# A transformer block, forward and backward: forward attention by chunks of 512 queries, the MLP of a chunk issued inside the next chunk's attention

## The chip, the cores and the metric

One core of one Trainium2 chip. The time is the device time of one launch in microseconds. Lower is better.

## The reference

One block on x of 2048 positions and 512 channels: attention with 32 heads of 16, and an MLP of 1792 hidden units with a squared ReLU. Both are modulated by six vectors from c. The kernel returns the output and the gradients of the nine inputs that take part.

```
mod = (silu(c) @ w_mod).reshape(1, 6, 1, -1)       # sa, ca, ga, sb, cb, gb
h = layernorm(x) * (1 + ca) + sa
q, k, v = split(h @ wqkv)                          # 32 heads of 16
x = x + ga * ((softmax(q @ k.T * 16**-0.5) @ v) @ wo)
h = layernorm(x) * (1 + cb) + sb
r = relu(h @ w1 + b1)
x = x + gb * ((r * r) @ w2 + b2)
out, vjp = jax.vjp(block, x, wqkv, wo, w1, b1, w2, b2, c, w_mod)
return out, *vjp(grad_out)
```

## The kernel before

Matmul operands are bfloat16, sums are float32 in PSUM, and positions are tiled by 128 (S, 16 tiles) or by 512 (four chunks). A quad is four heads whose 16 channels are padded to 32, so that a quad fills 128 partitions; there are eight. The program runs in stages, one behind the other:

- phase0: the six modulation vectors.
- phase12: first LayerNorm (x is loaded on SP's queue, L313), transposes, the V products (tm_group) and Q, K of quad 0 (fm_group: four matmuls of 512 columns, L281), then forward attention. The loop is over 16 pairs of heads, and within a pair over the four chunks of 512 queries, and within that over 16 blocks of 128 keys: 1024 units. A unit is two QK matmuls (L410) into a score buffer `st` of 128x1024, one exp on ScalarE (L413), and eight PV matmuls of 17 columns (L419) into `accbank`. 64 groups of 16 units share a PSUM bank: at a group's end VectorE takes two reciprocals (L428) and two products (L429), casts the group's output (L433) and clears the accumulator for the next group (L406). Three buffers hold scores. 120 further Q, K, V groups are put between the units at even steps. K comes to the chip once for each quad (L469), the masked Q per pair (L462), both on SP's queue. Each engine's order is the scheduler's.
- phase3: O is transposed on TensorE, then output projection (L523), second LayerNorm, fc1 (L547, with the ReLU on ScalarE, L549), square (L550), fc2 (L556).
- phase4: MLP backward: du (L652, with the product on VectorE, L654), dx (L661), the backward of the second LayerNorm (L578 to L590), dO (L940) and the padded, transposed copies of dO for the attention backward (L943 to L970). The weights are first transposed on TensorE (L570).
- phase45: weight gradients of the MLP and of wo; phase5: attention backward; phase6: the gradients through QKV and the modulation.

The operations of phases 3 and 4 depend on the attention's output of all heads of a position, and of nothing else in the attention.

Of the kernel before, what the change touches and what calls it, by code (L numbers as in the profile page):

```python
# [23 lines left out]
def chunks(total, size):  # L24
    out = []
    s = 0
    while s < total:
        w = min(size, total - s)
        out.append((s, w))
        s += w  # L30
    return out


class K:
# [29 lines left out]
    def build(self, ctx: ExitStack):  # L64
# [21 lines left out]
        self.stash = False  # L86
        if self.stash:
            self.put_d = self.dram("put_d", [NQ * 2 * self.SC * ST, P, 2, 512], BF16)

        stop = self.opts.get("stop_after", 99)  # L90
        self.dmaq = [nc.gpsimd]
        self.dmai = 0
        self.open_pools = {}
        phases = [self.phase0, self.phase12, self.phase12b, self.phase3, self.phase4, self.phase45, self.phase5, self.phase6, self.phase7]
        for i, ph in enumerate(phases):
            ph()
            if stop <= i:
                break
        for name in list(self.open_pools)[::-1]:
            self.close_pool(name)  # L100

    def phase12b(self):
        pass
# [11 lines left out]
    def phase0(self):  # L115
# [13 lines left out]
        self.e16 = pp.tile([P, 1], F32, name="e16")  # L129
        self.e1617 = pp.tile([P, 1], F32, name="e1617")  # L130
        nc.vector.memset(self.e16[:], 0.0)
        nc.vector.memset(self.e1617[:], 0.0)
        one11 = pp.tile([1, 1], F32, name="one11")
        nc.vector.memset(one11[:], 1.0)
        for j in range(4):
            nc.sync.dma_start(self.e16[32 * j + 16:32 * j + 17, :], one11[:])
            nc.sync.dma_start(self.e1617[32 * j + 16:32 * j + 17, :], one11[:])
            nc.sync.dma_start(self.e1617[32 * j + 17:32 * j + 18, :], one11[:])
# [7 lines left out]
        self.selmaskV = pp.tile([P, 64], F32, name="selmaskV")  # L146
        nc.gpsimd.memset(self.selmaskV[:], 0.0)
        for j in range(4):
            nc.gpsimd.affine_select(
                out=self.selmaskV[32 * j:32 * j + 16, :], in_=self.selmaskV[32 * j:32 * j + 16, :],  # L150
                compare_op=ALU.not_equal, fill=1.0, base=-16 * ((j + 2) % 4), pattern=[[1, 64]], channel_multiplier=-1)

        self.mod_bc = pp.tile([P, 6 * D], F32, name="mod_bc")
# [3 lines left out]
        with tc.tile_pool(name="p0", bufs=1) as sb, tc.tile_pool(name="p0ps", bufs=2, space=PSUM) as ps:  # L157
            cT_b = sb.tile([P, DT], BF16, name="cT_b")
# [19 lines left out]
            for (n0, nw) in chunks(6 * D, 512):  # L178
                pt = ps.tile([P, 512], F32, name="modps")
                for kt in range(DT):  # L180
                    nc.tensor.matmul(pt[:, :nw], lhsT=sc_bc[:, kt, :], rhs=wmod[:, kt, n0:n0 + nw],
                                     start=(kt == 0), stop=(kt == DT - 1))
                nc.vector.tensor_copy(self.mod_bc[:, n0:n0 + nw], pt[:, :nw])
            junk = sb.tile([P, P], F32, name="junk")
            for j in range(6):
                for t in range(DT):
                    nc.vector.scalar_tensor_tensor(
                        junk[:], self.mod_bc[:, j * D + t * P:j * D + (t + 1) * P], 1.0, self.ident_f[:],
                        ALU.mult, ALU.mult, accum_out=self.modT[:, j * DT + t:j * DT + t + 1])
        self.opcaT = pp.tile([P, DT], F32, name="opcaT")  # L190
# [3 lines left out]
        if "mod_bc" in self.dbg:  # L194
            nc.sync.dma_start(self.dbg["mod_bc"], self.mod_bc[:])
            nc.sync.dma_start(self.dbg["modT"], self.modT[:])

    def mod_row(self, j):
        D = self.D
        return self.mod_bc[:, j * D:(j + 1) * D]  # L200
# [53 lines left out]
    def phase12(self):  # L254
        tc, nc, pp, io = self.tc, self.nc, self.pp, self.io
        S, D, H, NQ, ST, DT = self.S, self.D, self.H, self.NQ, self.ST, self.DT
        self.rstd1 = pp.tile([P, ST], F32, name="rstd1")
        self.rl = pp.tile([P, ST, H], F32, name="rl")
        KB = ST
        po = self.open_pool("pO", bufs=1)  # L260
        self.O_tm = po.tile([P, ST, D], BF16, name="O_tm")
        self.wo_3 = po.tile([P, DT, D], BF16, name="wo3")
        with tc.tile_pool(name="p12", bufs=1) as sb, tc.tile_pool(name="p12e", bufs=8) as eb:
            xhat1T = sb.tile([P, DT, S], BF16, name="xhat1T")
            Vaug = sb.tile([P, ST, H, DH + 1], BF16, name="Vaug")
            nc.gpsimd.memset(Vaug[:, :, :, DH:DH + 1], 1.0)
            wq = sb.tile([P, DT, 3 * D], BF16, name="wqkv")
            nc.scalar.dma_start(wq[:], io["A_wqkv"].rearrange("(kt p) n -> p kt n", p=P))
            bias_bc = sb.tile([P, 3 * D], F32, name="bias_bc")
            bcol = sb.tile([P, 3 * NQ], F32, name="bcol")  # L270
            wpads = [sb.tile([P, DT, NQ, P], BF16, name=f"wpad{t}") for t in range(3)]
            for t in range(3):
                nc.gpsimd.memset(wpads[t][:], 0.0)
            dsts = [self.QTq_d, self.KTq_d, self.VTq_d]
            qtm_v = self.by_quad(self.qtm_d)
            ktm_v = self.by_quad(self.ktm_d)

            def fm_group(ps_pool, t, g, s0, sw, eng="vector"):
                pt = ps_pool.tile([P, 512], F32, name="pps")
                for kt in range(DT):  # L280
                    nc.tensor.matmul(pt[:, :sw], lhsT=wpads[t][:, kt, g, :], rhs=xhat1T[:, kt, s0:s0 + sw],  # L281
                                     start=(kt == 0), stop=(kt == DT - 1))
                ev = eb.tile([P, 512], BF16, name="ev_fm")
                bc = bcol[:, t * NQ + g:t * NQ + g + 1]
                if eng == "scalar":
                    nc.scalar.activation(ev[:, :sw], pt[:, :sw], ACT.Identity, bias=bc, scale=1.0)
                else:
                    nc.vector.tensor_scalar(ev[:, :sw], pt[:, :sw], bc, None, ALU.add)  # L288
                dq = self.dmaq[self.dmai % len(self.dmaq)]
                self.dmai += 1  # L290
                dq.dma_start(dsts[t][g, :, s0:s0 + sw], ev[:, :sw])

            def tm_group(ps_pool, st, t):
                pt = ps_pool.tile([P, 512], F32, name="pps")
                for kt in range(DT):
                    nc.tensor.matmul(pt[:, :D], lhsT=xhat1T[:, kt, st * P:(st + 1) * P], rhs=wq[:, kt, t * D:(t + 1) * D],
                                     start=(kt == 0), stop=(kt == DT - 1))
                if t < 2:
                    ev = eb.tile([P, D], BF16, name="ev_tm")
                    nc.vector.tensor_tensor(ev[:], pt[:, :D], bias_bc[:, t * D:(t + 1) * D], ALU.add)  # L300
                    dq = self.dmaq[self.dmai % len(self.dmaq)]
                    self.dmai += 1
                    with nc.allow_non_contiguous_dma(reason="128B runs"):
# [1192 lines left out]
```

## Time and profile before

| | |
|---|---|
| median of three runs | 3326.37 us (3326.18 to 3335.05) |
| profiled execution | 3329.45 us, its span 3327.6 us |
| granted TensorE clock, mean | 0.963 |
| busy: TensorE, VectorE, ScalarE, GpSimd | 2954.7, 1866.0, 2381.2, 231.7 us |
| startup, until the first exp | 0 to 93.3 us |
| forward attention, first to last exp | 93.3 to 1037.9 us |
| projection, MLP forward and backward, dO | 1037.9 to 1478 us |
| weight gradients | 1478 to 1653 us |
| attention backward | 1653 to 3153 us |

A line of the groups reads: code line, engine, operation, output and inputs by their names, count, then busy time and mean duration of one, then the idle time before it and what ended it. PEld is the loading of a matmul's stationary operand. Matmuls are pipelined: one of 512 columns is shown as 0.38 us, but in a run they follow one another sooner.

### The profile page before, as it was taken

The numbers are of one execution on the slowest core, as the hardware profiler recorded it, in microseconds if no ns is written. First come the engines' busy times: TensorE is split into PE (matmuls) and PEld (weight loads), VectorE is DVE, ScalarE is ACT, GpSimd is POOL, SyncE is SP. The second block draws the span as 40 slices with busy tenths as digits, with TensorE's granted clock in tenths as the row PEclk, the third lists the DMA queues.
The fourth block names the chain that finished last, engine by engine and source line by source line (L and its number), as shares of the span: only waits on it lengthen the run. The fifth ranks groups of instructions, "written<-read, shape, count | busy, mean of one in ns | idle before, by whom it ended". The sixth has DMA issues, their size and how long they took to land. (4 is left out here: it accounts for less than half of the span.)

```text
span 3327.6 us, 75207 instructions
## 1 busy us (share of the span) xinstructions
PE 2954.7 (89%) x31556; PEld 1438.8 (43%) x31556; DVE 1866.0 (56%) x2745; ACT 2381.2 (72%) x3577; POOL 231.7 (7%) x303
## 2 busy tenths in 40 slices
PE   5999998888885878849899999999999999999987
PEld 2455553333332334326544444444444444444433
DVE  6222220000001545626588888888888888888765
ACT  3899999999996223433377777777777777777633
POOL 3111220000002002431000000000000000000000
PEclk8999999999997889969999999999999999999998
DMA  3111110000004246564499999999999999999951
GB/s 124 64 51 48 46 51 12 6 13 12 6 2 146 81 141 203 138 203 148 130 192 189 203 187 206 193 204 195 192 201 190 206 191 205 191 188 184 206 170 62
DMA packets 1176799, 447.77 MB, mean 135 GB/s; under 512 B 1086346, under 2 KB 1142284, under 8 KB 1176460
## 3 DMA queue, kind: packets, MB, share of 16 engines
q1 hardware_dynamic: 1150556, 376.25, 56.3%
q0 software_dynamic: 17280, 57.03, 5.5%
q10 hardware_dynamic: 8624, 9.70, 0.9%
q8 instruction: 246, 4.03, 0.5%
q14 instruction: 93, 0.76, 0.1%
HBM read 106.83 MB, written 67.64 MB: 52 GB/s over the span
## 5 line engine op out<-in xcount | busy, mean ns | idle before, releaser
L1213 ACT ACTIVATE pu<-st 128x512 bf16<-128x512 f32 x2048 | 1132.7, 597 | 299.9 <-PE st L1211 298.1
L1218 DVE TENSOR_TENSOR ds<-dp,pu 128x1024 bf16<-128x1024 f32 x1024 | 1208.5, 1219 | 234.9 <-ACT pu L1213 226.9
L413 ACT ACTIVATE pu<-st 128x1024 bf16<-128x1024 f32 x1024 | 940.1, 1381 | 4.7 <-PE accbank L419 4.7
L1211 PE MATMUL st<-KTm,QTq 128*128 128x512 bf16 x2048 | 779.2, 380 | 14.9 <-ACT pu L1213 9.2
L1214 PE MATMUL dp<-VTm,dOTq 128*128 128x512 bf16 x2048 | 775.7, 379 | 7.5 <-DVE ds L1218 5.8
L1159 PEld LDWEIGHTS <-dsT 128*128 128x128 bf16 x8192 | 487.3, 96 | 490.3 <-DMA dsT<-ds 18.9
L410 PE MATMUL st<-QTm,KTq 128*128 128x512 bf16 x2048 | 606.9, 377 | 7.3 <-DMA KTq<-KTq_d 1.6
L1159 PE MATMUL accq<-Kg,dsT 128*128 128x16 bf16 x8192 | 493.7, 170 | 12.4 <-DMA dsT<-ds 12.3
L419 PEld LDWEIGHTS <-pu 128*128 128x128 bf16 x8192 | 291.9, 96 | 457.9 <-ACT pu L413 407.3
L419 PE MATMUL accbank<-Vaug,pu 128*128 128x17 bf16 x8192 | 353.9, 172 | 67.2 <-DVE accbank L406 7.5
L428 DVE RECIPROCAL rl<-accbank 128x4 f32<-128x4 f32 x128 | 23.0, 180 | 526.1 <-PE accbank L419 525.6
L1139 PE MATMUL acckv<-ds,Qg 128*16 128x512 bf16 x2048 | 309.1, 382 | 0.8 <-DVE ds L1218 0.7
L1139 PE MATMUL acckv<-pu,dOg 128*16 128x512 bf16 x2048 | 309.1, 382 | 0.0
L1211 PEld LDWEIGHTS <-QTq 128*128 128x128 bf16 x2048 | 196.0, 96 | 225.4 <-issue 220.6
L1214 PEld LDWEIGHTS <-dOTq 128*128 128x128 bf16 x2048 | 197.5, 96 | 36.1 <-DVE ds L1218 16.2
L288 DVE TENSOR_SCALAR ev_fm<-pps,bcol 128x512 bf16<-128x512 f32 x92 | 69.1, 751 | 195.9 <-PE pps L281 194.9
L410 PEld LDWEIGHTS <-KTq 128*128 128x128 bf16 x2048 | 130.0, 96 | 35.8 <-issue 20.5
L281 PE MATMUL pps<-xhat1T,wpad 128*128 128x512 bf16 x384 | 122.8, 378 | 4.9 <-DVE ev_fm L288 3.8
L1390 POOL DMA_DIRECT2D wmod<-in_w_mod_dram x6 | 4.5, 754 | 1553.7 <-DMA dsT<-ds 1519.8
L549 ACT ACTIVATE rT<-ups,bias 128x512 bf16<-128x512 f32 x56 | 38.5, 687 | 53.8 <-PE ups L547 53.8
L652 PE MATMUL daps<-gT,W2gbT 128*128 128x512 bf16 x224 | 58.5, 404 | 19.3 <-DVE duT L654 19.3
L725 ACT COPY a_blk<-trps 128x1024 bf16<-128x1024 bf16 x28 | 28.3, 1012 | 59.0 <-PE trps L722 58.9
(297 smaller groups left out, 2315.4 us busy)
## 6 DMA issues: line engine op xcount, KB each, us to landing
rT_d<-rT SPq DMA_DIRECT2D x4, 1792.0 KB
rT<-rT_d SPq DMA_DIRECT2D x4, 1792.0 KB
duT_d<-duT POOLq DMA_DIRECT2D x4, 1792.0 KB, 13.1
rT_f<-rT_d SPq DMA_DIRECT2D x14, 512.0 KB
duT_f<-duT_d POOLq DMA_DIRECT2D x14, 512.0 KB, 3.6
xhat_d<-xhat SPq DMA_DIRECT2D x2, 2048.0 KB
QTq_d<-ev_fm POOLq DMA_DIRECT2D x32, 128.0 KB, 2.1
QTm<-QTq_d SPq DMA_DIRECT2D x128, 32.0 KB
```

Source lines behind the costliest of these rows:

```text
L281: nc.tensor.matmul(pt[:, :sw], lhsT=wpads[t][:, kt, g, :], rhs=xhat1T[:, kt, s0:s0 + sw], start=(kt == 0), stop=(kt == DT - 1))
L288: nc.vector.tensor_scalar(ev[:, :sw], pt[:, :sw], bc, None, ALU.add)
L410: nc.tensor.matmul(stt[:, a, :qw], lhsT=KT[:, kb * P:(kb + 1) * P], rhs=QTm[a][:, q0:q0 + qw], start=True, stop=True)
L413: nc.scalar.activation(pu[:, :, :qw], stt[:, :, :qw], ACT.Exp, scale=self.scale)
L419: nc.tensor.matmul(acc[:, a, sub, :], lhsT=pu[:, a, sub * P:(sub + 1) * P], rhs=Vaug[:, kb, heads[a], :], start=False, stop=False, skip_gr ...
L652: nc.tensor.matmul(pt[:, :sw], lhsT=W2gbT[:, kt, ft * P:(ft + 1) * P], rhs=gT[:, kt, s0:s0 + sw], start=(kt == 0), stop=(kt == DT - 1))
L1139: nc.tensor.matmul(acckv[r:r + DH, :], lhsT=T[n][:, ib, col:col + DH], rhs=src[:, a, :], start=(ib == 0), stop=(ib == ST - 1))
L1159: nc.tensor.matmul(accq[:, ib, a, :], lhsT=dsT[:, (i * 2 + a) * 4 + sub, :], rhs=T["K"][:, 4 * c + sub, col:col + DH], start=(c == 0 and i ...
L1211: nc.tensor.matmul(stt[:], lhsT=T["QT"][:, q], rhs=masked["KT"][2 * jp + a][:, c0:c0 + 512], start=True, stop=True)
L1213: nc.scalar.activation(pu[:, a, :], stt[:], ACT.Exp, scale=self.scale)
L1214: nc.tensor.matmul(dp[:, a, :], lhsT=T["dOT"][:, q], rhs=masked["VT"][2 * jp + a][:, c0:c0 + 512], start=True, stop=True)
L1218: nc.vector.tensor_tensor(dsg[:, i], dp[:], pu[:], ALU.mult)
```

## The change

phase12, phase3 and phase4 become one stage, phase_fwd. Its loop is over four chunks of queries, within a chunk over the eight quads and their two pairs, and within a pair over the 16 blocks of keys: the same 1024 units, with all heads of a chunk done after 256 of them. TensorE's order is now written by hand: QK of unit n, PV of unit n−2, then a step of background work, which hands out matmuls from generators at a credit of 1.15 a unit. A generator can ask for a hold of some units (`yield ("wait", 9)`) to let an operand arrive. The background of chunk 0 is Q and K of quads 1 to 7; then the MLP weights; then, behind chunk c+1's attention, the whole of phases 3 and 4 for chunk c (260 matmuls of 512 columns). The last chunk's comes after the loop.

Other differences: `st` has two buffers instead of three, the background three PSUM banks. The transposes of O, of the normalised activations, of g, dx, dO and of the weights, and the position-major copies of Q, K and V, are DMA transposes on SP's queue instead of TensorE transposes or second products. V's padded product falls away. In hidden chunks ReLU, the LayerNorm backward and the scaling of the weights are VectorE's, and parts GpSimd's; in the last chunk ReLU and a part of the LayerNorm backward are ScalarE's, as before. K is loaded for each chunk and quad, 32 times instead of 8, and Q for each group; both on GpSimd's queue. The load of x stands in a pool that follows phase0's.

```diff
+class Background:
...
+    def step(self, rate):
+        if self.hold:
+            self.hold -= 1
+            return
+        self.credit = min(self.credit + rate, 2.0)
+        while self.gens and self.credit > 0:
+            r = self.next()
+            if r is None:
+                break
+            if isinstance(r, tuple):
+                self.hold = r[1]
+                break
+            self.credit -= max(r, 0.25)
...
-        phases = [self.phase0, self.phase12, self.phase12b, self.phase3, self.phase4, self.phase45, self.phase5, self.phase6, self.phase7]
+        phases = [self.phase0, self.phase_fwd, self.phase45, self.phase5, self.phase6]
...
+        def load_q(qc, g, jp):
+            for j in (2 * jp, 2 * jp + 1):
+                nc.gpsimd.dma_start(QTm[j][32 * j:32 * j + 32, :], self.QTq_d[g, 32 * j:32 * j + 32, 512 * qc:512 * (qc + 1)])
...
+        order = [(qc, g, jp) for qc in range(SC) for g in range(NQ) for jp in range(2)]
+        bg = Background()
+        bg.add(self.gen_qkv())
...
+        def pv(u):
+            (qc, g, jp, kb, acc, pu) = u
+            if kb == 0:
+                nc.vector.memset(acc, 0.0)
...
+            if (g, jp) == (NQ - 1, 1):
+                bg.add(self.gen_mlp(qc, self.take_o(qc, O32)))
...
+        with tc.manual_schedule(engines={mybir.EngineType.PE}):
+            for n, (qc, g, jp) in enumerate(order):
+                if (qc, g, jp) == (1, 0, 0):
+                    bg.drain()
+                    self.close_qkv()
+                    self.open_mlp()
+                    bg.add(self.gen_weights())
+                acc = accbank[:, n % 2]
+                for kb in range(ST):
+                    if kb == ST // 2 and n + 1 < len(order):
+                        load_q(*order[n + 1])
+                        if jp == 1:
+                            KTn = load_k(order[n + 1][1])
+                    stt = stp.tile([P, 2, 512], F32, name="st")
...
+                    nc.scalar.activation(pu[:], stt[:], ACT.Exp, scale=self.scale)
+                    pend.append((qc, g, jp, kb, acc, pu))
+                    if len(pend) > 2:
+                        pv(pend.pop(0))
+                    bg.step(1.15)
...
+        bg.drain()
+        self.close_mlp()
...
+    def gen_mlp(self, sc, O_b):
...
+        nc.sync.dma_start_transpose(OT[:].rearrange("p a b c -> p (a b) c"), O_b[:].rearrange("p a b -> p (a b)"))
...
+        nc.sync.dma_start_transpose(xhT[:].rearrange("p a b c -> p (a b) c"), xh[:].rearrange("p a b -> p (a b)"))
+        nc.gpsimd.dma_start(tm_v(self.xhat2_d), xh[:])
+        yield ("wait", 9)
...
+            if last:
+                nc.scalar.activation(rT[:, ft, :], pt[:], ACT.Relu, bias=self.bias1[:, ft:ft + 1], scale=1.0)
+            else:
+                nc.vector.tensor_scalar(rT[:, ft, :], pt[:], self.bias1[:, ft:ft + 1], 0.0, ALU.add, ALU.max)
...
+            if k:
+                yield from self.gen_do(sc, *todo.pop(0))
+        yield ("wait", 9)
+        yield from self.gen_do(sc, *todo.pop(0))
```

The order of instructions shows it at three places. First TensorE within a unit of the attention. Before, the two QK matmuls wait for an earlier PV (through the score buffer), and PV for the exp:

```order
L410 LDWEIGHTS KTq
L410 MATMUL st<-QTm_663,KTq 128x512 [waits PE_49]
L410 LDWEIGHTS KTq
L410 MATMUL st<-QTm_665,KTq 128x512
L419 LDWEIGHTS pu [waits Activation_49]
L419 MATMUL accbank<-Vaug,pu 128x17
...
```
After (auT is the squared ReLU, pps a background sum, L648 is fc2):

```order
L345 LDWEIGHTS KTq
L345 MATMUL st<-QTm_662,KTq 128x512 [waits Activation_49]
L345 LDWEIGHTS KTq
L345 MATMUL st<-QTm_664,KTq 128x512
L315 LDWEIGHTS pu
L315 MATMUL accbank<-Vaug,pu 128x17
...
L648 LDWEIGHTS auT
L648 MATMUL pps<-w_4901,auT 128x512
```
The wait for the exp has moved to the QK, a unit's PV comes after it without one, and a background matmul closes the unit.

Second, VectorE at a group's end. Before:

```order
L428 RECIPROCAL rl<-accbank 128x4 [waits DVE_49,PE_49]
L429 TENSOR_TENSOR O_660<-accbank,rl 128x4x16 [waits DVE_49]
L428 RECIPROCAL rl<-accbank 128x4
L429 TENSOR_TENSOR O_660<-accbank,rl 128x4x16 [waits DVE_49]
L433 CAST O_tm<-O_660 128x4x32 [waits DVE_49]
L406 MEMSET accbank 128x136
```
After, in the stretch where a hidden chunk's LayerNorm backward runs (lnb_nc to dx and dxb are its steps, dOp_t is dO):

```order
L702 TENSOR_SCALAR lnb_nc_8723<-lnb_s_8721 128x1 [waits DVE_49]
L704 TENSOR_SCALAR lnb_nc1r<-lnd_mv,rstd_5391 128x1 [waits DVE_49]
L706 SCALAR_TENSOR_TENSOR lnb_t<-xh_5608,lnb_nc_8723,pps 128x512 [waits DVE_49]
L322 RECIPROCAL rl<-accbank 128x4 [waits PE_49]
L709 SCALAR_TENSOR_TENSOR dx_8715<-lnb_t,rstd_5391,lnb_gp 128x512 [waits DMAHW2_49,DVE_49,Pool_49]
L323 TENSOR_TENSOR O_656<-accbank,rl 128x4x16 [waits DVE_49]
L681 CAST dxb<-dx_8715 128x512 [waits DMAHW1_49,DMASW3_49,DVE_49]
L322 RECIPROCAL rl<-accbank 128x4
L323 TENSOR_TENSOR O_656<-accbank,rl 128x4x16 [waits DVE_49]
L311 MEMSET accbank 128x136 [waits DVE_49]
L724 TENSOR_TENSOR dOp_t<-pps,rl 128x512 [waits PE_49]
```
The group's eviction and the clearing of the accumulator now stand between steps of the LayerNorm backward, one of which waits for GpSimd, and the cast of the group's output is gone.

Third, the queues at the start. SP before:

```order
L177 DMA wmod<-in_w_mod_dram 128x4x3072
...
L137 DMA e_91<-one_94 1x1 [waits DMAHW4_49]
L138 DMA e_91<-one_94 1x1 [waits DMAHW5_49]
L313 DMA x_269<-in_A_x_dram 128x16x512 [waits DMAHW6_49]
L316 DMA xhat_d<-xhat_271 128x16x512 [waits DMAHW0_49,Activation_49]
```
and after:

```order
L188 DMA wmod<-in_w_mod_dram 128x4x3072
L384 DMA x_246<-in_A_x_dram 128x16x512 [waits DMAHW0_49,DVE_49,DMAHW1_49,PE_49,Activation_49]
L387 DMA xhat_d<-xhat_248 128x16x512 [waits Activation_49]
L445 DMA QTq_d<-ev_fm 128x512 [waits DVE_49]
L447 DMA_TRANSPOSE ev_tm<-ev_fm 128x4x128
```
The load of x now waits for VectorE, ScalarE and TensorE. GpSimd's queue after, ahead of the first load of K (vpad is the padded copy of V, ktm_d the position-major K):

```order
L451 DMA ktm_d<-ev_tmc 128x256 [waits DMASW3_49,Pool_49]
L465 COPY vpad_228<-Vaug 128x8x2x16 [waits DMAHW5_49,DVE_49]
L466 COPY vpad_228<-Vaug 128x8x2x16
L465 COPY vpad_229<-Vaug 128x8x2x16 [waits DMAHW6_49,DVE_49]
L466 COPY vpad_229<-Vaug 128x8x2x16
L465 COPY vpad_228<-Vaug 128x8x2x16 [waits DMAHW7_49,DVE_49,Pool_49]
L466 COPY vpad_228<-Vaug 128x8x2x16 [waits Pool_49]
L468 DMA VTq_d<-vT 128x8x512 [waits DMAHW0_49]
L300 DMA KTq<-KTq_d 128x2048 [waits DMAHW1_49,DMASW5_49,DMAHW3_49,DVE_49,Activation_49]
```
In before the first load of K stands on SP's queue, right behind the first loads of Q.

More of the change, by code (lines that the diff above doesn't have):

```diff
@@ L258, in phase12 @@
         self.rl = pp.tile([P, ST, H], F32, name="rl")
[L259 to L267, printed above, removed]
-            nc.scalar.dma_start(wq[:], io["A_wqkv"].rearrange("(kt p) n -> p kt n", p=P))
[L269 to L279, printed above, removed]
```

1038 lines of the change are left out of this document (392 added, 646 removed).

## The prediction, made before the result was known

> **What bounds the kernel now.** I first read the busy time by stretches of the span, cut where the exps of the forward attention begin and end, where the MLP backward begins, where the weight gradients begin, and where the attention backward begins. Columns: length, then busy time and instruction count of each engine, the granted TensorE clock, the DMA share and GB/s.
>
> ```profile
> span 3327.6 us, 75207 instructions
> ...
> 0.00:93.30 93.30, 49.15 (x218) 21.75 (x219) 56.64 (x212) 29.57 (x37) 29.53 (x36) 0.84 0.38 128
> 93.30:1037.90 944.60, 867.46 (x10690) 398.66 (x10689) 155.44 (x495) 939.88 (x1024) 74.43 (x117) 1.00 0.08 26
> 1037.90:1236.00 198.10, 137.26 (x720) 63.07 (x720) 74.13 (x160) 55.16 (x71) 21.64 (x21) 0.84 0.43 149
> 1236.00:1478.00 242.00, 158.67 (x905) 79.33 (x906) 129.04 (x326) 90.91 (x213) 71.26 (x86) 0.81 0.60 179
> 1478.00:1653.00 175.00, 154.21 (x1632) 108.36 (x1630) 97.28 (x179) 55.52 (x55) 27.56 (x33) 0.98 0.43 132
> ```
>
> The second row is the forward attention: ScalarE, the fourth pair of numbers, is busy 939.88 of 944.60 us. The third and fourth rows are the phases for the output projection and MLP forward, and for the MLP backward: 198.1 + 242.0 = 440.1 us in which ScalarE is busy 146 us only. The two kinds of work stand one behind the other, and the change lays the second under the first. So the question is what room TensorE has in the attention. That is in the groups and in the timeline (start, duration, engine, line; in brackets the idle time before).
>
> ```profile
> L413 ACT ACTIVATE pu<-st 128x1024 bf16<-128x1024 f32 x1024 | 940.1, 1381 | 4.7 <-PE accbank L419 4.7
> ...
> L419 PEld LDWEIGHTS <-pu 128*128 128x128 bf16 x8192 | 291.9, 96 | 457.9 <-ACT pu L413 407.3
> ```
>
> ```profile
> 504.62 0.27 PEld L419 LDWEIGHTS <-pu 128*128 128x128 bf16 x8 [0.60 <-ACT pu L413]
> ...
> 504.84 0.59 PE L410 MATMUL st<-QTm,KTq 128*128 128x512 bf16 x2
> ...
> 505.54 0.27 PEld L419 LDWEIGHTS <-pu 128*128 128x128 bf16 x8 [0.60 <-ACT pu L413]
> ...
> 505.76 0.59 PE L410 MATMUL st<-QTm,KTq 128*128 128x512 bf16 x2
> ```
>
> The 1024 exps take 940.1/1024 = 0.918 us each, back to back, and a unit (one block of keys for a pair of heads and 512 queries) repeats in 505.54 − 504.62 = 0.92 us. TensorE waits for the exp's result in 407.3 us of the stage. Its eight PV matmuls take 504.84 − 504.62 = 0.22 us. A 512-wide matmul's issue time comes from a long run of them:
>
> ```profile
> 75.47 7.07 PE L281 MATMUL pps<-xhat1T,wpad 128*128 128x512 bf16 x32
> ```
>
> One alone takes 0.38, so (7.07 − 0.38)/31 = 0.216 us each. A unit thus holds TensorE for 0.22 + 2 × 0.216 = 0.65 us and leaves 0.27.
>
> **The change, term by term.** *Removed:* the 440.1 us stretch, of which a part comes back as the last chunk's tail.
>
> *Credit of 1.15 background matmuls a unit.* 0.65 + 1.15 × 0.216 = 0.90 us against 0.918: it fits, with 0.02 us to spare. ScalarE would go on setting the pace, but TensorE has next to nothing to catch up with. A stall in its queue that goes beyond the finished score tile ahead of ScalarE is paid in full. That tile is worth 0.918 − 0.59 (two QK matmuls) − about 0.08 (two semaphore gaps) = 0.25 us. Chunk 0's Q, K groups (224 matmuls) and three chunks of MLP (260 each), 1004 in all plus the bias ones, fit into 1024 × 1.15 = 1178 credits, so I expect all three to be done, but for the last four matmuls, when the attention ends.
>
> *Group boundary, 64 of them.* Before has it too, and this is what it looks like there:
>
> ```profile
> 524.79 0.36 PE L419 MATMUL accbank<-Vaug,pu 128*128 128x17 bf16 x8
> ...
> 525.20 0.19 DVE L428 RECIPROCAL rl<-accbank 128x4 f32<-128x4 f32 x1 [13.41 <-PE accbank L419]
> 525.42 0.23 DVE L429 TENSOR_TENSOR O<-accbank,rl 128x64 f32<-128x64 f32 x1
> 525.56 0.17 DVE L428 RECIPROCAL rl<-accbank 128x4 f32<-128x4 f32 x1
> ...
> 525.77 0.22 DVE L429 TENSOR_TENSOR O<-accbank,rl 128x64 f32<-128x64 f32 x1
> ...
> 526.02 0.23 DVE L433 CAST O_tm<-O 128x128 bf16<-128x128 f32 x1
> 526.28 0.17 DVE L406 MEMSET accbank<- 128x136 f32 x1
> ```
>
> The last PV run is issued by 524.79 + 0.22 = 525.01; the memset that the next PV waits for ends at 526.45. The chain is 1.44 us, and without the cast (0.26), which the change drops, 1.2 us. Before covers it with two further QK pairs from a third score buffer. After has two score buffers, and between the two PV runs stand only one background step (0.25) and one QK pair (0.43): 0.68. The stall is 1.2 − 0.68 = 0.5 us, of which the finished tile takes up between 0 and 0.25; I take 0.4, since at 0.02 us a unit the tile is only just rebuilt by the next boundary. 63 × 0.4 = **25 us**, with ends 0 (VectorE faster at it) and 35.
>
> *VectorE queue at boundaries.* VectorE now also works for the MLP, in order. Prices from before's MLP stretch:
>
> ```profile
> L654 DVE SCALAR_TENSOR_TENSOR duT<-daps,rT 128x512 bf16<-128x512 f32 x56 | 38.4, 688 | 29.3 <-PE daps L652 16.6 <-DMA rT<-rT_d 12.3
> ...
> L948 POOL TENSOR_TENSOR prod<-dOp_t,o 128x512 f32<-128x512 bf16 x16 | 18.8, 1172 | 0.3
> ...
> L587 DVE SCALAR_TENSOR_TENSOR lnb_t<-xch,lnb_nc,lnb_dxh 128x512 f32<-128x512 bf16 x16 | 15.9, 992 | 0.3
> ...
> L581 DVE SCALAR_TENSOR_TENSOR lnb_junk<-lnb_dxh,xch 128x512 f32<-128x512 f32 x16 | 13.8, 864 | 11.2 <-ACT lnb_dxh L578 11.2
> L590 DVE SCALAR_TENSOR_TENSOR dx<-lnb_t,rstd,lnb_gp 128x512 f32<-128x512 f32 x16 | 12.7, 794 | 12.9 <-DMA dx_d<-dx 11.5 <-ACT lnb_gp L589 0.6
> ...
> L212 DVE BATCH_NORM_STATS2 ln_stats<-x 128x6 f32<-128x512 f32 x16 | 10.6, 669 | 0.0
> ...
> L217 DVE TENSOR_SCALAR xhat<-x,ln_mv,rstd 128x512 bf16<-128x512 f32 x16 | 7.4, 541 | 0.0
> ...
> L505 ACT ACTIVATE w<-w,opcbT 128x1792 bf16<-128x1792 bf16 x4 | 6.8, 1776 | 11.5 <-PE b1ps L488 11.5
> ```
>
> Where LN2's backward runs, a tile costs VectorE 0.67 + 0.86 + 0.99 + 0.79 = 3.3 us, plus a wait for a GpSimd pass near 1.17, and the order of the change weaves the eviction into it. Some 3 boundaries of each hidden chunk fall there; at 2.5 us each, 3 × 3 × 2.5 = **22 us** (ends 0, where the tile lies clear of the boundary, and 9 × 4.5 = 40). Elsewhere the background's VectorE work (0.69 us for four matmuls, which take 3.2 us) has room.
>
> *Waits of TensorE for a transposed operand.* TensorE's order is fixed, so a late operand also holds QK. The price of a DMA transpose is only in the attention backward:
>
> ```profile
> L1225 SPq DMA_TRANSPOSE dsT<-ds x256: 4699/5106/6867, 1662.8 to 3141.0; - x128
> ...
> L1159 PEld LDWEIGHTS <-dsT x76: 95/96/98, 1672.3 to 1684.8; 128*128 128x128 bf16 x76
> ```
>
> 32 blocks of 128x128 take 5.1 us of queue, 0.16 us a block, and the first was usable at most 1672.3 − 1662.8 = 9.5 us after its issue, so at most 4.4 after the queue's part. For the second LayerNorm's operand (16 blocks): add, statistics and four normalisations 0.7 + 0.9 + 4 × 0.54 = 3.8 us, then 2.6 + up to 4.4: 11 us against the 9 units (8.3 us) that the code holds back. That is up to 2.7 us, three times. The scaling of w1, once, is four passes near 1.78 us in front of a boundary: 7 us. Together I take **15 us** (0 to 30).
>
> The Trainium skill, "VectorE: DVE Perf Modes", section "The three transpose paths", speaks against moving transposes off TensorE: it gives 1309 ns for a 128x128 block by DMA and 390 ns on TensorE. The row above, 0.16 us a block in a run of 32, is eight times below that.
>
> *Startup.* In before the load of x is issued at 14.53, and the first exp comes at 93.3:
>
> ```profile
> 14.53 0.39 SPq L313 DMA_DIRECT2D x<-in_A_x_dram  x1
> ...
> 25.11 0.68 DVE L245 BATCH_NORM_STATS2 ln_stats<-x 128x6 f32<-128x512 bf16 x1
> ...
> 86.01 0.35 SPq L469 DMA_DIRECT2D KTq<-KTq_d  x1
> ...
> 91.29 1.47 PE L410 MATMUL st<-QTm,KTq 128*128 128x512 bf16 x6 [1.56 <-DMA KTq<-KTq_d]
> ```
>
> After, the load waits for work of VectorE, ScalarE and TensorE that in before ends about where the statistics start (25 us), so LayerNorm starts some 12 us later. K is then loaded by GpSimd's queue, behind copies that wait for the first transposes; Q and K are computed before V now, which gives some of it back. I take **+15 us** (0 to 25).
>
> *Tail.* Behind the last exp stand the last chunk's 260 matmuls and 4 left over: 264 × 0.216 = 57 us at full clock. Around them nothing fills TensorE: O's eviction, cast and transpose 8 us, LN2 and its transpose 10, the last LN backward, transpose and dO 9; and part of it runs at the lower clock that the MLP stretches had (0.81, 0.84), which I put at 4. **88 us.** Lower end 70 (full clock, weight gradients starting early), upper end 440.1/4 = 110, before's own price of a quarter.
>
> *Unchanged:* from the weight gradients on (1478 to the end) the code is the same. *Moved off for nothing:* TensorE's transposes and V groups, hidden behind the exp or gone with the 440 us.
>
> The profiled execution took 3329.45 us: 3329.45 − 440 + 25 + 22 + 15 + 15 + 88 = 3054; the median of the runs shown is 3 us below this execution, so **3051 us**.
>
> **Rivals.** *A: TensorE paces the loop.* With 0.02 us spare, a tenth of a microsecond more per unit (semaphore gaps of the fixed order, matmuls held by a product whose VectorE eviction is late) is not hidden: 1024 × 0.1 = 102 us, so 3153. For it: the spare is small, and there are two score buffers in place of three. Against it: in the attention backward TensorE runs as densely:
>
> ```profile
> 1653.00:3153.00 1500.00, 1452.58 (x16644) 704.04 (x16645) 1257.00 (x1113) 1151.40 (x2084) 1.81 (x3) 0.99 1.08 196
> ```
>
> 1452.58 of 1500 us at a granted clock of 0.99. Chance 0.20.
>
> *B: the stalls vanish.* VectorE's work falls clear of the boundaries, startup costs 5, the tail 75, stalls 15: 3326 − 440 + 95 = 2981. Against it: the chain above is a row, not a guess. Chance 0.16.
>
> *C: slower than before.* Each hidden chunk has five places where TensorE must wait for a transposed operand (the LN2 product, and four dO groups), the tail six: 21 in all. To eat 3326 − 3051 = 275 us, each must wait 13 us longer than in the sum, so a transpose would be some 22 us late instead of 9.5; at 25 us the kernel stands at 3051 + 21 × 16 = 3387. Queued behind one another and behind stores on one queue they might be that late; the DMA engines' share of 0.08 in the attention speaks against it. Chance 0.05. A milder form, 4 us longer each, gives 3051 + 84 = 3135; chance 0.05.
>
> By the page's 1309 ns, 16 blocks would take 20.9 us in place of 2.6, so the LN2 product would wait 18 us longer in each of four chunks, and O's transpose in the tail as much: 90 us, an estimate by that page, 3141. The row's 9.5 us for twice the blocks is against it.
>
> *D: no gain.* If the loads of Q and K, now in GpSimd's queue, are held there each time, all 64 groups lose; to lose the whole 275 us each would have to lose 4.3 us. The load is asked for 8 units (7.3 us) ahead and a transfer of that queue lands 2.0 us after its issue:
>
> ```profile
> KTq_d<-ev_fm POOLq DMA_DIRECT2D x32, 128.0 KB, 2.0
> ```
>
> So a hold of 7.3 − 2.0 + 4.3 = 9.6 us at every group would be needed. Chance 0.02.
>
> **How the numbers follow.** The forecast, 3020 to 3085, has 0.52. The range for 8 in 10 takes in B's centre and the lower half of A: 2980 to 3140. A measurement of this kernel tells 0.3% (10 us) from no change. Faster: 0.52 + 0.20 + 0.16 + 0.05 = 0.93; within 0.3%: 0.02 (D); slower: 0.05 (C).
>
> **What would show it.** Right: the exps span 985 to 1025 us in place of 944; idle time before the exp is put down to PV and memset, once in 16 exps; no MLP matmul but the last chunk's after the last exp; 80 to 95 us from there to the first weight gradient. First exp near 108. Wrong: gaps before the exp spread evenly over the units (A), long waits of TensorE for a DMA transpose (C) or for Q and K (D), or a change in the time of the attention backward.

## The result: 3142 us, 0.944 of the time before

The changed kernel takes 3142.47 us in the median of four runs (3136.24 to 3143.60), against 3327.52 for the kernel before (3326.18 to 3335.05): a ratio of 0.9436, 95% interval 0.9417 to 0.9455. The forecast of 3051 had the direction and the mechanism; the gain is 185 us where 275 were expected (3326 − 3051), and the time lies 57 us above the forecast's 3020 to 3085 and 2 us above the upper end of the wide range, 3140.

The profile after, in stretches (length, busy time and count of TensorE, weight load, VectorE, ScalarE, GpSimd; clock, DMA share, GB/s), cut at the first and the last exp of the forward attention, behind the last dO product, and shortly behind the first weight-gradient products:

```profile
0.00:104.30 104.30, 44.14 (x199) 19.58 (x203) 52.27 (x178) 29.84 (x36) 31.51 (x59) 0.76 0.50 145
104.30:1132.50 1028.20, 923.09 (x11079) 514.61 (x11281) 297.78 (x854) 959.51 (x1025) 225.28 (x419) 0.98 0.37 94
1132.50:1252.70 120.20, 66.89 (x268) 26.95 (x272) 51.62 (x142) 17.69 (x31) 24.64 (x40) 0.78 0.57 122
1252.70:1290.20 37.50, 12.41 (x43) 8.37 (x45) 17.97 (x31) 7.33 (x16) 18.79 (x18) 0.54 0.83 258
1290.20:1458.30 168.10, 144.56 (x1584) 102.82 (x1596) 92.26 (x164) 51.26 (x40) 15.21 (x26) 1.00 0.44 130
```

The attention stretch is 1028 us long where it was 945, and ScalarE is no longer busy in all of it. The groups of that stretch say why:

```profile
L348 ACT ACTIVATE pu<-st 128x1024 bf16<-128x1024 f32 x1024 | 959.6, 1041 | 68.7 <-PE st L345 57.7
...
L315 PE MATMUL accbank<-Vaug,pu 128*128 128x17 bf16 x8192 | 359.1, 171 | 64.6 <-DVE accbank L311 57.7
```

The exp waits 57.7 us for scores (4.7 us in all before), and PV waits 57.7 us for the memset of the accumulator. That the two sums are equal is chance; where the exps lose time has to be counted. I take 0.9165 us as the exp's own pace and add up by how much more than that lies between the ends of successive exps. The whole lag is 89.7 us, of which 59.2 us fall on one place, exp number 3 of a group of 16, counted from 0. PV runs two units late, so this is the exp behind the first QK that stands behind the new group's first PV. (By its place it is the group's fourth; the expectations below, and this text from here on, call it the third exp of a group.) In the kernel before the same count gives 6.2 us, 6.1 of them at that place.

The span adds up as follows, with each stretch against the same stretch before (the attention backward's first exp is at 1655.5 before, 1458.3 after):

| stretch | before | after | difference | forecast |
|---|---|---|---|---|
| up to the first exp | 93.3 | 104.3 | +11 | +15 |
| first to last exp | 944.8 | 1028.3 | +83.5 | +62 |
| last exp to the attention backward | 617.4 | 325.7 | −291.7 | −352 (−440 + 88) |
| attention backward | 1484.1 | 1493.6 | +9.5 | 0 |
| rest | 187.9 | 189.8 | +1.9 | 0 |

The third row holds two thirds of the miss. TensorE's own view of it (start, duration, what it did; in brackets the wait before it):

```profile
1135.62 1.89 PE L720 MATMUL pps<-wogaT,dxT 128*128 128x512 bf16 x4 [2.59 <-DMA dxT<-dxb]
1147.26 0.61 PE L616 MATMUL pps<-wo,fT 128*128 128x512 bf16 x1 [9.75 <-DMA fT<-O_b]
...
1168.75 13.56 PE L635 MATMUL pps<-fT,w 128*128 128x512 bf16 x56 [16.06 <-DMA fT<-xh]
...
1231.41 1.89 PE L720 MATMUL pps<-wogaT,dxT 128*128 128x512 bf16 x4 [17.19 <-DMA dxT<-dxb]
...
1247.67 1.89 PE L720 MATMUL pps<-wogaT,dxT 128*128 128x512 bf16 x4 [5.92 <-DMA dxT<-dxb]
...
1266.95 2.01 PE L826 MATMUL csbps<-diag,ones_f 128*128 128x128 f32 x6 [14.27 <-DVE dsb_part L846]
1279.30 6.96 PE L826 MATMUL csbps<-diag,ones_f 128*128 128x128 f32 x22 [10.35 <-DVE diag L824]
1286.05 0.63 PE L769 MATMUL g2ps<-g_tm,ones_b 128*128 128x512 bf16 x1
```

From the last exp to the last dO product are 120 us instead of 88, and then 37 us pass before the weight gradients are under way.

### The profile page after: what moved, and what is told of

Its sections match the earlier page's. It is cut to its first block, busy times and chain, and to the rows that moved or that the text cites. A ratio compares the mean times of both kernels' runs of the same rounds, so it can differ in the third digit from the quotient of the medians.

```text
span 3141.7 us, 73207 instructions
## 1 busy us (share of the span) xinstructions
PE 2765.5 (88%) x30278; PEld 1440.6 (46%) x30788; DVE 1866.1 (59%) x2741; ACT 2274.9 (72%) x3325; POOL 322.8 (10%) x569
## 5 line engine op out<-in xcount | busy, mean ns | idle before, releaser
L348 ACT ACTIVATE pu<-st 128x1024 bf16<-128x1024 f32 x1024 | 959.6, 1041 | 68.7 <-PE st L345 57.7
L1019 PE MATMUL dp<-VTm,dOTq 128*128 128x512 bf16 x1779 | 675.5, 380 | 7.9 <-DVE ds L1023 5.9
L345 PE MATMUL st<-QTm,KTq 128*128 128x512 bf16 x1938 | 592.9, 382 | 48.9 <-issue 13.8
L315 PEld LDWEIGHTS <-pu 128*128 128x128 bf16 x8192 | 355.3, 96 | 318.0 <-issue 86.5
L315 PE MATMUL accbank<-Vaug,pu 128*128 128x17 bf16 x8192 | 359.1, 171 | 64.6 <-DVE accbank L311 57.7
L345 PEld LDWEIGHTS <-KTq 128*128 128x128 bf16 x2048 | 193.0, 96 | 205.0 <-issue 147.2
L1019 PEld LDWEIGHTS <-dOTq 128*128 128x128 bf16 x2048 | 197.6, 96 | 36.6 <-DVE ds L1023 16.2
L444 DVE TENSOR_SCALAR ev_fm<-pps,bcol 128x512 bf16<-128x512 f32 x60 | 45.0, 751 | 152.9 <-PE pps L436 87.8
L296 POOL DMA_DIRECT2D QTm<-QTq_d x128 | 64.8, 509 | 444.1 <-PE st L345 400.4
L661 DVE SCALAR_TENSOR_TENSOR auT<-pps,rT 128x512 bf16<-128x512 f32 x56 | 38.7, 692 | 95.6 <-PE pps L659 83.2
L635 PE MATMUL pps<-fT,w 128*128 128x512 bf16 x224 | 72.9, 384 | 20.7 <-DMA fT<-xh 20.7
L641 DVE TENSOR_SCALAR rT<-pps,bias 128x512 bf16<-128x512 f32 x42 | 31.5, 751 | 93.9 <-PE pps L635 93.8
```

The source lines that it names most:

```text
L296: nc.gpsimd.dma_start(QTm[j][32 * j:32 * j + 32, :], self.QTq_d[g, 32 * j:32 * j + 32, 512 * qc:512 * (qc + 1)])
L315: nc.tensor.matmul(acc[:, a, sub, :], lhsT=pu[:, a, sub * P:(sub + 1) * P], rhs=Vaug[:, kb, h, :], start=False, stop=False, skip_group_che ...
L345: nc.tensor.matmul(stt[:, a, :], lhsT=KT[:, kb * P:(kb + 1) * P], rhs=QTm[2 * jp + a][:], start=True, stop=True)
L348: nc.scalar.activation(pu[:], stt[:], ACT.Exp, scale=self.scale)
L444: nc.vector.tensor_scalar(ev[:], pt[:], bc, None, ALU.add)
L635: nc.tensor.matmul(pt[:], lhsT=self.w1[:, kt, ft * P:(ft + 1) * P], rhs=xhT[:, :, kt, :], start=(kt == 0), stop=(kt == DT - 1))
```

## The experiments

Chips differ a little, so a kernel is compared with the runs of before on its own chip.

### Whose lag is it in the loop: two accumulator banks

The accumulators of two successive groups are halves of one PSUM bank. The first PV into one half waits for its memset, and the memset stands in VectorE's queue behind the eviction of the other half. The experiment changes two things together: each accumulator gets a bank of its own, and it is cleared half a group ahead:

```diff
-        accbank = accp.tile([P, 2, 2, 4, DH + 1], F32, name="accbank")
+        accb = [accp.tile([P, 512], F32, name=f"accbank{i}") for i in range(2)]
+        accs = [t[:, 0:8 * (DH + 1)].rearrange("p (a s d) -> p a s d", a=2, s=4) for t in accb]
...
-        self.mps = self.open_pool("mps", bufs=3, space=PSUM)
+        self.mps = self.open_pool("mps", bufs=2, space=PSUM)
...
-            if kb == 0:
-                nc.vector.memset(acc, 0.0)
...
+            if kb == ST // 2:
+                nc.vector.memset(accs[(jp + 1) % 2], 0.0)
```

> The two accumulator halves get a PSUM bank each (the background keeps two banks instead of three), and the next group's half is cleared in the middle of the group before, so that no PV waits for the eviction. Theory (the eviction chain of VectorE between two groups is what delays the exps: 59 us of the 90 us by which the exps lag their own pace, all at the third exp of a group): the lag at that place falls from 59 to under 8 us, the exps span about 975 us instead of 1028, and the kernel takes 3085 to 3100. Rival (TensorE's tight pace with two score buffers is the cause, and the lag only shows there): the lag moves to other units and the time stays above 3125.

Measured: 3085.63 us, ratio to before 0.9264 (0.9250 to 0.9278). The lag at the third exp fell from 59.2 to 1.3 us, the whole lag from 90 to 33, and the exps span 972 us. The same two groups:

```profile
L350 ACT ACTIVATE pu<-st 128x1024 bf16<-128x1024 f32 x1024 | 952.7, 1045 | 19.2 <-PE st L347 17.1 <-ACT pu L350 0.5
...
L314 PE MATMUL accbank<-Vaug,pu 128*128 128x17 bf16 x8192 | 358.2, 171 | 7.2 <-ACT pu L350 0.6 <-issue 0.2
```

PV no longer waits for VectorE at all. The chain between two groups was the cause. Whether the bank of its own or the early clearing would have done alone was not tried. The Trainium skill, "Perfetto Trace Analysis", section "Matmuls", advises rotating independent matmul groups through different PSUM banks so that one's evacuation overlaps the next one's matmuls; this run agrees: with the early clearing, the lag fell by 58 us over 63 boundaries. The control of this run takes away only the background's third bank:

> The changed kernel with two PSUM banks for the background's products instead of three, nothing else: the part of the first of these runs that is not the eviction. Theory: an eviction takes 0.7 us and a product 3.2 us in the loop, so two banks do: within 8 us of 3142. Rival: the third bank absorbs VectorE's late evictions, and the loop is 20 us longer or more.

It took 3136.56 us in its one run, with 59 us of PV's wait for the memset as in the changed kernel. The gain is the accumulator's.

### Or TensorE's pace: a lower credit

```diff
-                    bg.step(1.15)
+                    bg.step(1.0)
```

> The changed kernel with a credit of 1.0 background matmuls a unit instead of 1.15, nothing else. TensorE's work per unit falls from 0.90 to 0.87 us against the exp's 0.918. Theory (the boundary chain sets the loop, not TensorE's pace): the lag at the third exp of a group stays at 45 to 60 us, the exps span 1010 to 1030 us, some 100 matmuls of the third chunk's MLP spill behind the loop, and the kernel takes 3155 to 3170. Rival (TensorE's pace sets the loop): the exps' span shortens by 30 us or more and the kernel is not slower than 3142.

Measured: 3168.28 us in one run. The exps span 1018.7 us, ten less, the lag at the third exp is still 55.2 us, and the stretch from the last exp to the attention backward grew from 325.7 to 361.5 us. At this credit TensorE's pace is worth about 10 us of the loop, and the work that spills costs 36 us behind it. It is one run, but in the kernels with the old credit and one accumulator bank the exps span 1026 to 1032 us.

### Is it the MLP that makes the evictions late: MLP exposed

```diff
-                    bg.step(1.15)
+                    if qc:
+                        bg.drain()
+                    else:
+                        bg.step(1.15)
```

> Same chunk order, but from chunk 1 on the background is not spread over the units: each chunk's MLP is issued in one piece at the start of the next chunk, as the last one's is. What is left in the loop is attention alone. Theory (the chain recip, product, recip, product, memset against a cover of one QK pair costs 0.5 to 0.7 us at every boundary, MLP or not): some 25 to 40 us of lag at the third exp of a group remain, and the kernel takes 3142 + 3 x 120 - 40 = about 3460. Rival (the MLP's own VectorE work makes the evictions late): under 10 us remain there, and about 3440. If hiding cost far more than the 84 us seen in the loop, this kernel would be within 200 us of the changed one.

Measured: 3426.17 us in one run, its span 283 us above the changed kernel's, and 34 us below the theory's time: the three exposed pieces cost 113 us each instead of 120, and other waits of the loop went with the MLP. Hiding three chunks is worth 94 us a chunk.

The lag at the third exp is 27.7 us, inside the theory's 25 to 40, but that is luck, as the count by chunk shows:

| lag at the third exp, us | chunk 0 | chunk 1 | chunk 2 | chunk 3 |
|---|---|---|---|---|
| changed kernel | 11.1 | 13.3 | 20.9 | 13.9 |
| MLP exposed | 16.6 | 3.7 | 3.7 | 3.7 |

Chunk 0 has the Q, K background in both kernels, and one late exp of 5.4 us in this run. In the other three chunks the MLP's removal takes 48 us down to 11, 0.23 us a boundary. So with nothing but attention in the loop the bare chain costs less than the theory's 0.5 to 0.7. The run takes the MLP's matmuls away as well as its work on VectorE, so it doesn't say which of the two counts. The changed kernel's own boundaries tell more. At 25 of the 63 VectorE does nothing but the five steps, from 0.7 us ahead of the first reciprocal to the memset; there the exp is late by 0.46 us in the mean. At 18 boundaries it is late by more than 1 us, 36.3 us together, and at every one of them VectorE does background work in that stretch. At 0.46 for each of the 63, the bare chain would be 29 us and VectorE's other work the remaining 30, an estimate from these counts. Both kinds show in the timeline. A boundary at which VectorE was free:

```profile
767.59 0.18 DVE L322 RECIPROCAL rl<-accbank 128x4 f32<-128x4 f32 x1 [10.33 <-PE accbank L315]
767.81 0.23 DVE L323 TENSOR_TENSOR O<-accbank,rl 128x64 f32<-128x64 f32 x1
...
767.95 0.17 DVE L322 RECIPROCAL rl<-accbank 128x4 f32<-128x4 f32 x1
768.16 0.23 DVE L323 TENSOR_TENSOR O<-accbank,rl 128x64 f32<-128x64 f32 x1
768.49 0.17 DVE L311 MEMSET accbank<- 128x136 f32 x1
768.71 0.35 PE L315 MATMUL accbank<-Vaug,pu 128*128 128x17 bf16 x8 [0.28 <-DVE accbank L311]
```

and one in the dO part of a hidden chunk:

```profile
638.13 0.69 DVE L729 TENSOR_TENSOR lnb_junk<-dOp_t,o 128x512 f32<-128x512 bf16 x1 [2.70 <-DMA o<-O_d]
...
639.46 0.17 DVE L322 RECIPROCAL rl<-accbank 128x4 f32<-128x4 f32 x1
...
640.90 0.17 DVE L311 MEMSET accbank<- 128x136 f32 x1
641.12 0.36 PE L315 MATMUL accbank<-Vaug,pu 128*128 128x17 bf16 x8 [4.09 <-DVE accbank L311]
641.34 1.01 PE L345 MATMUL st<-QTm,KTq 128*128 128x512 bf16 x2
```

In the first the exp is 0.46 us late. In the second, VectorE itself waits 2.70 us for a load (O, read back for the row sums), with the eviction queued behind it, and TensorE then waits 4.09 us. Its granted clock, the third number from the end, falls with it:

```profile
637.00:638.90 1.90, 0.04 (x1) 0.00 (x0) 0.73 (x2) 1.23 (x2) 0.42 (x2) 1.00 1.21 203
639.00:641.10 2.10, 0.00 (x0) 0.00 (x0) 1.95 (x13) 0.00 (x0) 0.56 (x1) 0.50 1.22 265
```

The next QK pairs take 1.01 us in place of 0.59. The Trainium skill, "TensorE: Matmul & The Clock Gate", section "Part 1: The HAM clock gate", tells of such a half clock behind an idle window of some 3.4 us. The half clock is there in the trace, but it begins about 1.9 us after TensorE's last matmul, so the length of the window can't be read from this row.

The same count names the other heavy boundaries. Two of 4.0 us lie at the start of a chunk, where the cast of the finished chunk's O stands between the last eviction and the memset:

```profile
619.48 1.63 DVE L587 CAST O_b<-O 128x512 bf16<-128x512 f32 x4
621.14 0.17 DVE L311 MEMSET accbank<- 128x136 f32 x1
```

### What holds the tail: the store of du

TensorE waits 17.2 us for the transpose of the first dx, and the timeline has the largest store of the tail (du, 1792 KB) just ahead of it. The edit puts that store, in the last chunk, behind the dx loop in the program.

> In the last chunk alone the 1792 KB store of du is issued behind the last dO instead of ahead of the dx products. Theory (the store fills the DMA engines, so that dx's transpose and the store of the first dx wait for it: 17.2 us of TensorE's wait in the tail): that wait falls below 6 us, the tail shortens by 10 to 15 us, and the kernel takes 3125 to 3135, unless the weight gradients then wait for du. Rival (the transpose is late by itself): the wait stays at 15 to 17 us, time 3142.

Measured: 3143.40 us (ratio 0.9437), and the wait was there again:

```profile
PE pps L723 <- DMA dxT<-dxb: 27.2, 4, 17.3
```

The edit hadn't moved the store on the chip: it was issued 1.0 us behind the last du product, as in the changed kernel (1209.21 there), next to another small one on SP's queue.

```profile
1214.02 1.10 POOL L690 DMA_DIRECT2D duT_d<-auT  x1 [11.66 <-DVE db L536]
```

```profile
1214.21 0.39 SPq L540 DMA_DIRECT2D out_dram<-db_b  x1
```

So this run tells nothing of du, but the stretch behind it in the changed kernel does (columns as above; the last two are DMA share and GB/s):

```profile
1210.00:1215.00 5.00, 4.22 (x20) 1.73 (x18) 2.39 (x6) 1.89 (x4) 0.65 (x2) 1.00 1.42 33
1215.00:1220.00 5.00, 0.00 (x0) 0.00 (x0) 1.64 (x5) 1.45 (x4) 1.30 (x3) 0.92 0.60 20
```

DMA engines that are busy and move 20 to 33 GB/s aren't simply full of a large store, which could be moved faster: 379 GB/s between 1225 and 1230. The trace's records of single packets show what is among them: 1792 packets of 2 bytes, the gradient of b1, written element by element from a column layout. Of the 4 KB packets that start between 1212 and 1222 half take more than 1.8 us, where the later ones take 0.16. The 2-byte packets' own records are 0.01 us each, so the records don't show how they would hold up the others; that they do is what the next run tests.

### The gradient of b1 by row

The weight-gradient stage makes the same vector as a row; it is stored from there:

```diff
-            nc.sync.dma_start(self.io["out_5"].rearrange("(t p) -> p t", p=P), db1_b[:])
...
+        nc.vector.tensor_copy(db1_b[:], db1_bc[0:1, :])
+        nc.sync.dma_start(io["out_5"].rearrange("(o f) -> o f", o=1), db1_b[:])
```

> The gradient of b1 is stored from the row form that the weight-gradient stage has anyway (one run of 3.5 KB), not as 1792 elements of 2 bytes right behind the last du product. The store of du stays where it was. Theory (the 2-byte store keeps all DMA engines for some 15 us, and the transpose of the first dx and its store stand behind it): TensorE's wait of 17.2 us for that transpose falls to 4 to 7 us, the wait of 12.2 us for the store of the first dx vanishes, the stretch from the last exp to the attention backward shortens by 10 to 14 us; kernel 3128 to 3134. Rival (the transpose is late by itself, in a tail that has nothing to hide it): the wait stays, no change of time.

Measured: 3130.87 us, ratio 0.9394 (0.9380 to 0.9408) where the changed kernel has 0.9436, some 14 us less; last exp to attention backward 315.7 us, 10 less. DMA issues (KB each, median us to landing) in the changed kernel; the stretch for dx holds its first store and transpose alone:

```profile
duT_d<-auT POOLq DMA_DIRECT2D x1, 1792.0 KB, 20.7
out_dram<-db_b SPq DMA_DIRECT2D x1, 3.5 KB, 15.7
...
dx_d<-dx SPq DMA_DIRECT2D x1, 256.0 KB, 15.0
...
dxT<-dxb SPq DMA_TRANSPOSE x1, 16.2
```

and with the row store, where du's store stands at the same place:

```profile
duT_d<-auT POOLq DMA_DIRECT2D x1, 1792.0 KB, 7.7
...
dx_d<-dx SPq DMA_DIRECT2D x2, 256.0 KB, 3.6
...
dxT<-dxb SPq DMA_TRANSPOSE x1, 3.9
```

```profile
1225.29 1.89 PE L716 MATMUL pps<-wogaT,dxT 128*128 128x512 bf16 x4 [4.91 <-DMA dxT<-dxb]
...
PE pps L716 <- DMA dxT<-dxb: 14.8, 4, 6.2
```

The wait for the first dx's transpose fell from 17.2 to 4.9 us, that for all of dx's transposes from 26.9 to 14.8. A store of 3.5 KB had held up 1792 KB.

### The start

x is loaded right behind w_mod into a buffer that doesn't follow the modulation's, and the first Q and K are asked for on ScalarE's queue.

```diff
+        nc.sync.dma_start(self.x0[:], io["A_x"][0].rearrange("(st p) d -> p st d", p=P))
...
-        load_q(0, 0, 0)
-        KT = load_k(0)
+        load_q(0, 0, 0, nc.scalar)
+        KT = load_k(0, nc.scalar)
```

> x is loaded right behind w_mod, before the modulation, into a buffer of its own, and the first Q and K go to the chip on ScalarE's queue instead of behind the copies on GpSimd's. Theory (the first exp is late by 13 us of LayerNorm and some 8 us of K's load, less what computing Q and K before V gave): first exp at 84 to 90 us instead of 104, kernel 3122 to 3128. Rival (only the order of the products matters): first exp above 98.

```profile
L351 ACT ACTIVATE pu<-st x1024: 1017/1030/1091, 89.3 to 1117.8; 128x1024 bf16<-128x1024 f32 x171
```

The first exp starts at 89.3 us instead of 104.3, near the late end of the forecast, and the kernel takes 3129.92 us, ratio 0.9392 (0.9374 to 0.9410), 2 us more than the forecast's 3122 to 3128. The two edits were run together, but the trace tells them apart in part: LayerNorm's first statistics start at 27.0 us instead of 38.4, and K's load is issued at 81.8 instead of 95.5. So 11 of the 15 us are the load of x. From the first statistics to K's load 54.8 us pass instead of 57.1, so the other queue gives some 2 us there, not the 8 of the forecast. What brings the first exp below the 93.3 of the kernel before was not taken apart.

### The start of the weight gradients

```diff
+        gp = self.open_pool("gtm", bufs=1)
+        self.g_tm = gp.tile([P, ST, D], BF16, name="g_tm")
         bg.drain()
...
+        if last:
+            nc.scalar.dma_start(self.g_tm[:], io["grad_out"][0].rearrange("(st p) d -> p st d", p=P))
```

> The attention's buffers are given back when the loop ends, and grad_out for the weight gradients (2 MB) is loaded into their place behind the last chunk's fc1 instead of at the stage's start. Theory (the 38 us between the last dO product and the first weight-gradient product are loads that can start only when the MLP's buffers are free, of which this 2 MB is the first): 8 to 15 us less, kernel 3127 to 3134. Rival (the other 2 MB load and the first rT and duT, which stay where they were, end last): no change, or later by the DMA time taken from the tail's transposes.

Measured: 3143.61 us, ratio 0.9433, no change. TensorE's waits tell why:

```profile
PE pps L620 <- DMA fT<-O_b: 15.5, 1, 15.5
PE csbps L831 <- DMA b_b<-in_B_b_dram: 9.5, 1, 9.5
```

In the program the load stands behind the last chunk's fc1. It went out at 1138.1, 7.5 us after the last exp, within 0.3 us of O's transpose, and took 15.1 us to land; the wait for O's transpose grew from 9.8 to 15.5 us. The stage then waits for its other loads. Which of these ends last was not taken further.

### All of it together

> All of it together: two accumulator banks with early clearing, b1's gradient by row, early loads of x, Q and K, and grad_out ahead of the stage. Theory (the parts lie one behind the other on the path and add up): 3142 - 56 - 12 - 17 - 11 = 3046, range 3036 to 3060. Rival (they cover each other): above 3065.

> Everything of the combined kernel but the early load of grad_out, which by itself gave nothing: it made O's transpose in the tail wait 15.5 us instead of 9.8. Theory: 0 to 8 us less than the combined kernel, 3060 to 3070 on a chip where before takes 3334, and the wait for O's transpose is back at 10 us. Rival (the early load helps once the 2-byte store is gone): 5 us or more above the combined kernel.

Measured: 3069.19 us (3066.52 to 3074.07) with the early load of grad_out, ratio to before 0.9212 (0.9197 to 0.9227), and 3074.13 us (3065.59 to 3075.06) without, 0.9215 (0.9200 to 0.9231). The two can't be told apart, so the second forecast, 3060 to 3070, was missed, though O's wait was back at 10.5 us. Either is some 2.4% faster than the changed kernel by its ratio. The first forecast, 3036 to 3060, was missed too, and the rival's bound of 3065 passed: the gain is less than the sum of the parts. Most of that lies in the loop, where the exps span 987 and 992 us and two banks alone had 972. The late exps are now few and single (up to 6 us each, most of them within the first 40 units, at the start of the second chunk, and at a transposed operand). In chunk 0 the lag rose from 9 to 17 us; with the early loads alone it rose too, from 22 to 28, so that the earlier start seems to give part of its gain back there. The other 7 to 11 us were not traced to a cause.

## Why the prediction was right or wrong

- **What bounds the loop, right.** ScalarE's exp at 0.918 us, TensorE just below. The lower credit moved the exps' span by 10 us only, and with two accumulator banks the same credit left a span of 972. So rival A (a tenth of a microsecond per unit, 102 us) did not happen, and that the total came near its 3153 is chance. The wide range was said to take in the lower half of A, but ended at 3140, so the measured time falls just outside.
- **Group boundary and VectorE's queue, right in mechanism and place, a little small.** Forecast 25 + 22 = 47 us over before; measured 59.2 − 6.1 = 53. By the estimate above the split is about 29 and 30 of the 59. The bare chain costs 0.46 us a boundary in the tight loop, near the 0.4 of the sum, and 0.23 where TensorE has room. And the LayerNorm backward is not the heaviest: a boundary in dO's part, with VectorE waiting for a load, cost 4.3 us, and the cast of a chunk's O, which the sum didn't have, stands at two of 4.0 us.
- **Other waits in the loop, mis-sized.** Forecast 15, measured 30 (89.7 − 59.2). TensorE waited 4.6 us for LN2's transposed operand there, where the sum had 8, and 5.1 us for loads of Q, which the sum had at nothing. The lower credit took about 6 of the 30 away; the rest was not split further.
- **Startup, right.** 11 us against 15.
- **The tail, wrong, 60 us.** The prediction expected 80 to 95 us from the last exp to the first weight gradient; it was 153. Two steps failed. First, the 440.1 us taken out ran to the first weight gradients, while the 88 us put back ended at the last dO product. Before has a gap there too, from 1453.8 on:

```profile
1459.57 1.01 PE L968 MATMUL trps<-ident,dOpad 128*128 128x128 bf16 x8 [5.75 <-ACT dOpad L965]
1476.91 1.04 PE L722 MATMUL trps<-ident,rT_f 128*128 128x128 bf16 x8 [16.33 <-ACT rT_f L714]
```

  It is 24 us there and 37.5 after, of which 9 come back in the stage itself (177.5 us before, 168.1 after, since the small products are done in the gap): 28 us that the sum had counted as removed. Second, the tail's own chain was 120 us, not 88. The gaps were put at 27 us and were 53: 16 for the second LayerNorm's operand (10 in the sum, 11 by the chain that the prediction itself worked out), 24 for the last dx and dO (9 expected), of which some 12 are the 2-byte store, 12 before and at O's transpose (8 expected). In the second LayerNorm, VectorE waits 2.98 us for a load of x, which the sum didn't have:

```profile
1157.43 0.69 DVE L618 TENSOR_TENSOR x<-pps,x 128x512 f32<-128x512 f32 x1 [2.98 <-DMA x<-in_A_x_dram]
```

  The matmuls, at a granted clock of 0.78, were 67 instead of 57 + 4. The upper end of that term, 110, a quarter of before's stretch, was also too low: before runs each step over all four chunks, which may be what fills such waits there; that was not tried.
- **Transposes: rival C did not happen in the loop, its milder form did in the tail.** In the loop TensorE waited less for them than the sum had. The tail's waits for a transposed operand were 26 us longer than in the sum, 4 us each over six; the one that landed late, dx's first at 16.2 us, was held up by the 2-byte store, and took 3.9 without it. The LN2 operand's 16 blocks were in use at 1168.75, 6.3 us after their issue:

```profile
1162.42 1.58 SPq L627 DMA_TRANSPOSE fT<-xh  x1
```

  By the Trainium skill, "VectorE: DVE Perf Modes", section "The three transpose paths", 1309 ns a block would make 20.9 us, an estimate from that page's figure. The trace disagrees for 16 blocks moved by one instruction.
- **Attention backward, +9.5 us.** Its code is the same, and over the other runs here it took 1482 to 1491 us, so most of this may be spread between runs; before has one trace only, 1484.

## What to carry to other kernels

When work is hidden under a loop, price what it does to the in-order engine that closes each round of that loop: before, two QK pairs ran while VectorE did its small steps, the second of them into a third score buffer; with two buffers the steps cost some 0.5 us at a typical boundary and up to 4.3 at a busy one, until the next accumulator lay in a bank of its own and was cleared ahead. When a stretch is taken out and its remainder put back, cut both at the same event, and price the remainder by its chain of waits, not by its busy time. In an exposed tail look at the DMA engines' share beside the GB/s: busy engines that move little were the sign of a store of single elements here.

## What the runs showed of the hardware that was not expected

A store of 1792 elements of 2 bytes, 3.5 KB in all, took 15.7 us to land, and beside it a store of 1792 KB took 20.7 us instead of 7.7, and a transpose of 128x512 16.2 instead of 3.9. TensorE's granted clock was down to 0.50 some 1.9 us after its last matmul. And a line that stands later in the program isn't issued later for that: the store of du left 1.0 us behind the last du product, also when its line stood behind the dx loop.
